# A fused attention and mixer block on one core: attention in 57-query blocks of 64 keys, large weights in pieces between the transposes, and a searched order of the blocks

## The chip, the cores and the metric

The kernel runs on one core of one Trainium2 chip. The metric is device time in microseconds (us), from runs most of which agree within 1.5%. The profiled execution is described by its *span*, which is about 2 us shorter than the time of the same run. "PE" is TensorE, "PEld" its weight loads, "DVE" VectorE, "ACT" ScalarE, "POOL" GpSimd and "SP" the engine whose queue issues nearly all DMAs. The *granted clock* is the share of full speed that TensorE was given. A run more than 1.5% above the fastest of its kernel is called slow here. The medians quoted are of all runs of a kernel.

## The reference

The input is `x` with 2048 tokens of 448 values, and all data are bf16. Two pre-norm blocks follow each other.

```python
def A(x, wqkv, wo):            # 16 heads of 28, window 8, dilation 2
    q, k, v = split(x @ wqkv)
    idx = pos[:, None] - arange(8)[None, :] * 2      # keys s, s-2, ..., s-14
    logits = einsum("bhsd,bhswd->bhsw", q, k[idx]) * 28**-0.5     # masked where idx < 0
    return einsum("bhsw,bhswd->bhsd", softmax(logits), v[idx]) @ wo

def B(x, w1, w2, w3, w4):      # w1, w2: 448x448, w3: 448x1792, w4: 1792x448
    h  = gelu(layernorm(x) @ w1)
    hs = shift_quarters(h) @ w2        # quarters of the columns moved by +1, -1, +2, -2 tokens
    x1 = x + hs
    return x1 + gelu(layernorm(x1) @ w3) @ w4

h  = x + A(layernorm(x), wqkv, wo)
h2 = h + B(layernorm(h), w1, w2, w3, w4)
```

## The kernel before

Because of the dilation, even and odd tokens never meet in the attention. The kernel keeps them apart as two "parities" (`a`) of 1024 positions, each query then seeing its own and the 7 keys before. Normalized tiles are transposed by DMA on the SP queue (`HT<-ln` in the trace) and feed the projections.

A block of the attention has 121 queries and 128 keys, so that the keys fill the partitions. Most of the 128x121 scores lie outside the window. They are computed and exponentiated, and then multiplied by a 0/1 mask. The four heads of a group use the four 32-row strips of the array.

```python
NQ = 121
def phase_att(g):                       # two windows w, one group c of four heads at a time
    for (c, a, w), o in cols.items():   # scores, 28 x 128 keys by 121 queries
        k0 = W0 + NQ * w - 7
        for j in range(4):
            ins.append(mm(Ts[j // 2](...), QK[r, 1, a, c, k0:k0 + nk], QK[r, 0, a, c, q0:q0 + nq], True, True))
    for jp in range(2):
        act(pj, Ts[jp](...), ACT.Exp, 2 * tot, scale=SCALE)
        dve("tensor_tensor", ..., out=pj, in0=pj, in1=mb, op=ALU.mult)      # the mask
    for (c, a, w), o in cols.items():   # probabilities times values, 128 keys by 32
        for j in range(4):
            ins.append(mm(T(...), vt[0:nk, w % NV, a, 4 * c + j, :], pt[0:nk, sl, j, o:o + nq], True, True))
    ...                                 # copy out, then norm(): denominators through DRAM, product
```

The weights are issued in one go, after the first four layer norms. W3 is two DMAs of 1568 KB and W4 is one of the same size:

```python
def weights():
    ...                                                    # wo, w1, w2
    wload("w3", w3_s[:], B_w3)
    dma("w4", w4_s[:], B_w4.rearrange("(f k) n -> k f n", k=128), D * F * 2)

setup()
for m in range(4): phase_LN1(m)
weights()
unit_qkv(0); phase_att(0); unit_qkv(1); ...
```

Nothing of this runs in program order. The program text builds a list of operations with durations, and a list scheduler in the kernel orders them for each engine. Of the ready operations it takes the one that can start first in its own model of the chip. Among operations that could start within a slack of that, it takes the one with the lower `prio`, which before the change is the place in the program text. All instructions are emitted by one helper, so every one carries the same line number in the profile, and groups are told apart by their tiles.

Of the kernel before, what the change touches and what calls it, by code (L numbers as in the profile page):

```python
# [15 lines left out]
class _Op:  # L16
    __slots__ = ("idx", "eng", "ins", "kw", "dur", "deps", "users", "sem", "val", "t0", "t1", "clock", "is_dma",
                 "chan", "lat", "odeps", "tag", "opts", "table", "prio", "groups", "mode", "xb")

    def __init__(self, idx, eng, ins, dur):  # L20
        self.idx = idx; self.eng = eng; self.ins = ins; self.dur = dur
        self.deps = set(); self.users = 0; self.sem = None; self.val = 0
        self.t0 = None; self.t1 = None; self.clock = None; self.xb = False
        self.opts = None; self.table = None; self.prio = idx; self.groups = []; self.mode = None
        self.is_dma = False; self.chan = None; self.lat = 0.0; self.odeps = set()
# [61 lines left out]
class _Sched:  # L87
# [11 lines left out]
    def macro(self, eng, ins, dur, chan=None, lat=0.0, opts=None, table=None, mode=None, after=()):  # L99
# [3 lines left out]
        if chan is not None:  # L103
            op.is_dma = True; op.chan = chan; op.lat = float(lat)
            self.chan_count[chan] = self.chan_count.get(chan, 0) + 1
            op.val = 16 * self.chan_count[chan]
# [62 lines left out]
    XLAT = 130.0  # L169
    TABLE = 1300.0  # L170
    MODE = 90.0

    def prepare(self):
# [16 lines left out]
        self.engs = sorted(set(e for op in self.ops for e in (op.opts or {op.eng: None})))  # L190

    def schedule(self, dma_bw=180.0, slack=100.0):
        if not hasattr(self, "children"):
            self.prepare()
        n = len(self.ops)
        children = self.children
        npend = list(self.npend)
        XLAT = self.XLAT
        ops = self.ops
        engs = self.engs  # L200
        holder = [None] * 8
        held_by = [[] for _ in range(8)]
        fin = [0.0] * n
        arr = [{} for _ in range(n)]
# [4 lines left out]
        def place(n, t, taken=()):  # L209
            best = None  # L210
            for b in range(0, 8, n):
                f = 0.0
                for x in range(b, b + n):
                    if holder[x] is not None or x in taken:
                        break
                    for o in held_by[x]:
                        if o.eng != "pe":
                            v = fin[o.idx] + XLAT
                            if v > f:
                                f = v  # L220
                else:
                    key = (max(f, t), 0 if n > 1 else -b, -f)
# [5 lines left out]
        base = [dict.fromkeys(engs, 0.0) for _ in range(0)]  # L228

        def push(op):  # L230
            at = {}
            for e in (op.opts or (op.eng,)):
                t = 0.0
                for d in op.deps:
                    i = d.idx
                    x = fin[i] + (0.0 if d.is_dma or eng_of[i] == e else XLAT)
                    if x > t:
                        t = x
                for d in op.odeps:
                    i = d.idx  # L240
                    if fin_start[i] > t and eng_of[i] != e:
                        t = fin_start[i]
# [4 lines left out]
        fin_start = [0.0] * n  # L247
# [8 lines left out]
        dma_free = 0.0  # L256
        done = 0
        MODE = self.MODE
        cands = {e: None for e in engs}
        dirty = set(engs)  # L260
        while done < n:
            best = None
            for e in engs:
                cand = None
                fr = free[e]
                for op in ready[e]:
                    st = arr[op.idx][e]
                    if st < fr:
                        st = fr
                    if cand is not None and st > cand[0] + slack:  # L270
                        continue
                    bad = False
                    if op.groups and e == "pe":
                        taken = ()
                        for g in op.groups:
                            if g not in gbank:
                                at = place(g.n, st, taken)
                                if at is None:
                                    bad = True
                                    break  # L280
                                if at[1] > st:
                                    st = at[1]
                                taken = taken + tuple(range(at[0], at[0] + g.n))
                        if bad:
                            continue
                    if e == "act" and op.table is not None and op.table != table:
                        st += self.TABLE
                    if cand is None or st < cand[0] - slack or (st < cand[0] + slack and op.prio < cand[1].prio):
# [11 lines left out]
            if e == "act" and op.table is not None:  # L300
                table = op.table
            if e == "pe":
                if op.mode != mode:
                    dur += MODE
                mode = op.mode
            op.t0 = st
            fin_start[i] = st
            for g in op.groups:
                if g not in gbank:
# [4 lines left out]
                    g.wait = set()  # L314
                    for x in range(b, b + g.n):
# [3 lines left out]
                    g.opener = op  # L319
                gleft[g] -= 1  # L320
                b = gbank[g]
                for x in range(b, b + g.n):
# [3 lines left out]
            if op.is_dma:  # L326
                free[e] = st + dur
                ts = max(st + dur, dma_free)
                dma_free = ts + op.lat / dma_bw
                op.t1 = dma_free + 2000.0  # L330
            else:
                op.t1 = st + dur
                free[e] = op.t1
# [4 lines left out]
            for ch in children[i]:  # L338
# [5 lines left out]
        return order  # L344
# [52 lines left out]
def _fast_path(nc, es, flag, A_x, A_wqkv, A_wo, B_w1, B_w2, B_w3, B_w4, out):  # L397
# [3 lines left out]
    NF, KB, NQ, W0 = 14, 7, 121, 8  # L401
# [16 lines left out]
    HT = sb("HT", [128, KB, 16 + 1024], BF16)  # L418
    QK = sb("QK", [128, 2, 2, 4, QW], BF16)
    NV = 5  # L420
    vt = sb("vt", [128, NV, 2, 16, 32], BF16)
    pt = sb("pt", [128, 3, 4, 4 * NQ], BF16)
    osb = sb("osb", [128, 3, 2, 512], F32)
    rzb = sb("rzb", [128, 2, 512], F32)
    zp = sb("zp", [128, 3, 32], F32)
    rzp = sb("rzp", [128, 3, 32], F32)
    msk = sb("msk", [128, 4 * NQ], BF16)
    xin = sb("xin", [128, 16, D], BF16)
    xb = sb("xb", [128, 16, D], BF16)
    NL = 3  # L430
# [16 lines left out]
    rz_d = nc.dram_tensor("rz_scratch", (9 * 4, 1024), F32, kind="Internal")  # L447

# [16 lines left out]
    def dma(chan, out_ap, in_ap, nbytes, dur=500.0):  # L465
        return S.add("sp", "dma_start", dur, chan=chan, lat=nbytes, out=out_ap, in_=in_ap)
# [16 lines left out]
    def wload(chan, dst, src):  # L483
        for u in range(2):
            dma(chan + "ab"[u], dst[half[u]], src.rearrange("(b k) n -> k b n", k=64),
                src.shape[0] * src.shape[1] * 2)
# [7 lines left out]
    def load_x(m):  # L494
        dma("x%d" % m, xin[:, 2 * m:2 * m + 2, :].rearrange("p a n -> p (a n)"), xrows(A_x, m), 128 * D * 4)

    def setup():
        S.tag = "setup"
        for m in range(2):
            load_x(m)  # L500
        for b0, b1 in ((0, 3), (3, 7)):
            wload("wqk%d" % b0, wst[:, b0:b1, :], A_wqkv[64 * b0:64 * b1, 0:2 * D])
        wload("wv", wv_s[:], A_wqkv[:, 2 * D:3 * D])
        for m in range(2, 8):
            load_x(m)
        pool("memset", 300, ap=mhalf[:], constant=-0.5)
        dve("memset", 100, ap=HT[:, :, 0:16], constant=0.0)
        dve("memset", 100, ap=QK[:, 1, :, :, 0:W0], constant=0.0)
        dve("memset", 100, ap=QK[:, 1, :, :, W0 + 1024:QW], constant=0.0)
        dve("memset", 400, ap=vt[:, :, :, :, 29:32], constant=0.0)  # L510
        dve("memset", 200, ap=vt[:, :, :, :, 28], constant=2.0 ** -4)
        dve("memset", 100, ap=vt[0:7, 0, :, :, 28], constant=0.0)
        dve("memset", 600, ap=msk[:], constant=1.0)
        m4 = msk[:].rearrange("p (b q) -> p b q", q=NQ)
        pool("affine_select", 600, out=m4, in_=m4, pattern=[[0, 4], [-1, NQ]], compare_op=ALU.is_ge, fill=0.0, base=0,
             channel_multiplier=1)
        pool("affine_select", 600, out=m4, in_=m4, pattern=[[0, 4], [1, NQ]], compare_op=ALU.is_ge, fill=0.0, base=7,
             channel_multiplier=-1)
        dve("memset", 70, ap=ones[:], constant=1.0)
        dve("memset", 70, ap=w1_s[:, KB * D:], constant=0.0)  # L520
        dve("memset", 1100, ap=osb[:], constant=1.0)
        dve("memset", 500, ap=wqk_p[:, :, :, 28:32], constant=0.0)
        pool("memset", 1600, ap=wo_s[:], constant=0.0)
        for c in range(4):
            for w in range(2):
# [3 lines left out]
                    "act": ([("activation", dict(ka, func=ACT.Copy))], 220 + 784 / 1.2),  # L529
                    "dve": ([("tensor_copy", ka)], 560)}, **ka)  # L530

    def weights():
        S.tag = "weights"
        wov = A_wo.rearrange("(c j d) n -> j d c n", c=4, j=4)
        for j in range(4):
            dma("wo%d" % j, wo_s[32 * j:32 * j + 28, :, :], wov[j], D * D * 2 // 4)
        wload("w1", w1_s[:, 0:KB * D].rearrange("p (b n) -> p b n", b=KB), B_w1)
        dma("w2", w2_s[:], B_w2.rearrange("(c k) n -> k c n", k=112), D * D * 2)
        wload("w3", w3_s[:], B_w3)
        dma("w4", w4_s[:], B_w4.rearrange("(f k) n -> k f n", k=128), D * F * 2)  # L540
# [3 lines left out]
    def ln_stats(kind, src, i):  # L544
        k = stc[0] % 8
        stc[0] += 1
        dve("bn_stats", 600, out=st6[:, k, :], in_=src)
        dve("bn_aggr", 180, out=mv[:, kind, i, :], in_=st6[:, k, :])

    def inv_std(slot, kind, i0, n, s1=1.0, s2=EPS):  # L550
        pool("tensor_scalar", 250, out=vtmp[:, slot, i0:i0 + n], in0=mv[:, kind, i0:i0 + n, 1], scalar1=s1,
             scalar2=s2, op0=ALU.mult, op1=ALU.add)
        pool("tensor_tensor", 400 + 164 * n, out=rstd[:, slot, i0:i0 + n], in0=vtmp[:, slot, i0:i0 + n],
             in1=mhalf[:, 0:n], op=ALU.pow)

    def normalize(slot, kind, i, out_ap, in_ap):
        dve("tensor_scalar", 400, out=out_ap, in0=in_ap, scalar1=mv[:, kind, i, 0:1],
            scalar2=rstd[:, slot, i:i + 1], op0=ALU.subtract, op1=ALU.mult)

    lctr = [0]  # L560

    def ln_to_HT(slot, kind, m, src):
        sl = lctr[0] % NL
        lctr[0] += 1
        for a in range(2):
            normalize(slot, kind, 2 * m + a, ln[:, sl, :, a, :], src[:, 2 * m + a, :].rearrange("p (b d) -> p b d", d=64))
        S.add("sp", "dma_start_transpose", 1400.0, chan=ch("tr"), lat=128 * 896 * 2,
# [765 lines left out]
```

## Time and profile before

| | before |
|---|---|
| time, median of 3 runs | 285.08 us |
| span of the profiled run | 280.3 us |
| first matmul | 21.6 us |
| PE busy | 192.5 us |
| PE idle between the first and the last matmul | 61.2 us |
| after the last matmul | 5.0 us |
| mean granted clock | 0.884 |

The head of the page of the kernel before: span, busy time by engine, then the busy tenths of PE and the granted clock in 40 slices of 7 us each.

```profile
span 280.3 us, 5851 instructions
...
PE 192.5 (69%) x2567; PEld 128.4 (46%) x2567; DVE 138.4 (49%) x296; ACT 102.0 (36%) x109; POOL 51.3 (18%) x92
...
PE   0009640699906540999999935569996489999892
...
PEclk9999955599986796699999977599999669999999
```

PE is the busiest engine. It is idle in the first three slices and has holes at slices 5 to 8, 12 to 16, 24 to 27 and 31 to 32, counted from 1. Below many of the holes, or just after them, the clock row drops to 5 to 7, so the idle time costs twice, since the work after it runs slower.

The waits of the kernel before, PE only: who ended the idle time, us in total, how many times, the longest.

```profile
PE ps L1259 <- DMA HT<-ln: 42.2, 3, 21.6
PE ps L1259 <- DVE pt L1259: 13.7, 6, 7.1
...
PE ps L1259 <- issue: 3.4, 2, 2.1
```

The transposes (`HT<-ln`) ended 42.2 us of PE's idle time in three waits, of which 21.6 us is the start. The masked probabilities (`DVE pt`) ended 13.7 us. The normalized attention (not shown) ended another 7.8 us.

The timeline of the kernel before: first of the SP queue, then of PE (start, length, what ran, and in brackets the idle time before it and what ended it).

```profile
24.72 27.08 SPq L1259 DMA_TRANSPOSE HT<-ln  x3
```

```profile
51.84 2.80 PE L1259 MATMUL ps<-wv_s,HT 64*128 64x448 bf16 x14 [9.75 <-DMA HT<-ln]
...
61.00 1.49 PE L1259 MATMUL ps<-wv_s,HT 64*128 64x448 bf16 x14
```

Three transposes issued from 24.7 us on kept the SP queue for 27.08 us (the first of them for 23.01), and most single ones later in the same trace take 1.22 to 1.25 us. They stood behind W3 and W4. The page lists those loads as three of 1568 KB with a median of 23.2 us to landing. The second and third lines show the value projection of a window after that wait, and the same work later. It took 2.80 us against 1.49 us, which is the price of a cold clock. The Trainium skill's page "TensorE: Matmul & The Clock Gate", Part 1, says the array runs at half clock until it has been busy for some 3.4 us. This pair, 1.9 to 1, agrees with the half clock.

The groups of the attention in the kernel before (line, engine, operation, tiles, shapes, count, busy us, mean ns, idle before).

```profile
L1259 ACT ACTIVATE pt<-ps 128x968 bf16<-128x968 f32 (+1 forms) x34 | 31.0, 976 | 6.5 <-PE ps L1259 6.5
L1259 DVE TENSOR_TENSOR pt<-pt,msk 128x968 bf16<-128x968 bf16 (+1 forms) x34 | 22.0, 653 | 24.8 <-ACT pt L1259 24.8
L1259 PE MATMUL ps<-pt,vt 128*32 128x121 bf16 (+1 forms) x288 | 8.1, 247 | 15.8 <-DVE pt L1259 13.7 <-ACT pt L1259 2.1
L1259 PE MATMUL ps<-QK 28*128 28x121 bf16 (+1 forms) x288 | 7.4, 226 | 3.0 <-DVE osb L1259 0.8 <-ACT pt L1259 0.7 <-ACT vt L1259 0.7
```

Exponentials and masks cost 31.0 us of ACT and 22.0 us of DVE. Those engines are busy 36% and 49% of the span.

### The profile page before, as it was taken

Reading aid. Unit: us, or ns where it says so; the run is one execution under the profiler, and the core shown is the slowest. Engines: PE = TensorE matmul, PEld = TensorE weight load, DVE = VectorE, ACT = ScalarE, POOL = GpSimd, SP = SyncE. Lnnn points to the kernel's source line nnn. Section 1 sums busy time; section 2 is a strip of 40 time slices with the busy share of each in tenths; the row PEclk is TensorE's granted clock in tenths of the full one; section 3 lists DMA queues with packets and bytes.
Section 4 is the critical chain, followed back from the end, with each engine's and each line's share of the span. In section 5 each row is a group of like instructions: output and inputs, shape, how many; then the busy total and the mean of one; then the engine's idle time right before and its main releaser. Section 6 shows DMA issues by size and latency. Waiting matters only on the chain.

```text
span 280.3 us, 5851 instructions
## 1 busy us (share of the span) xinstructions
PE 192.5 (69%) x2567; PEld 128.4 (46%) x2567; DVE 138.4 (49%) x296; ACT 102.0 (36%) x109; POOL 51.3 (18%) x92
## 2 busy tenths in 40 slices
PE   0009640699906540999999935569996489999892
PEld 0006420377505220765865622269553439857651
DVE  6857180207897587174824466682127764020020
ACT  0403870169653600236971670026201105603500
POOL 4414000000040023016400001731002547000000
PEclk9999955599986796699999977599999669999999
DMA  6999999822044234203110132321010313001001
GB/s 176 218 284 211 218 204 278 145 79 77 7 105 62 61 82 103 73 1 69 35 36 33 37 83 77 75 57 35 2 47 19 68 33 62 10 33 35 4 34 41
DMA packets 35341, 23.16 MB, mean 83 GB/s; under 512 B 25836, under 2 KB 33388, under 8 KB 35308
## 3 DMA queue, kind: packets, MB, share of 16 engines
q1 hardware_dynamic: 35308, 22.71, 35.8%
q8 instruction: 22, 0.36, 0.6%
q14 instruction: 11, 0.09, 0.1%
HBM read 15.09 MB, written 1.97 MB: 61 GB/s over the span
## 4 chain that ended last, share of the span: by engine, by line
PE 59%; DMA 17%; DVE 11%; ACT 6%; issue 3%; POOL 2%; SPq 1%; DVEq 0%
PE ps L1259 59%; DMA HT<-ln 15%; DVE st L1259 3%; ACT pt L1259 3%; DVE xb L1259 2%; DMA h<-in_A_wqkv_dram 2%; DVE xin L1259 2%; DVE QK L1259 1%; ACT QK L1259 1%; POOL rstd L1259 1%; SPq L1259 1%; DVE mv L1259 1%; DVE ln L1259 1%; ACT osb L1259 1%; ACT L1259 0%
## 5 line engine op out<-in xcount | busy, mean ns | idle before, releaser
L1259 PE MATMUL ps<-HT,w_s 64*128 64x256 bf16 (+1 forms) x1064 | 61.7, 279 | 19.2 <-DMA HT<-ln 10.8
L1259 PEld LDWEIGHTS ps<-HT,w_s 64*128 64x128 bf16 x1064 | 55.2, 101 | 25.8 <-DMA HT<-ln 16.2
L1259 DVE TENSOR_TENSOR xb<-ps,xb 128x448 bf16<-128x448 f32 (+1 forms) x24 | 18.6, 776 | 64.0 <-PE ps L1259 64.0
L1259 ACT ACTIVATE QK<-ps 128x1024 bf16<-128x1024 f32 (+2 forms) x24 | 22.7, 953 | 53.2 <-PE ps L1259 53.2
L1259 POOL TENSOR_SCALAR vtmp<-mv 128x2 f32<-128x2 f32 (+1 forms) x34 | 7.9, 233 | 175.2 <-DVE mv L1259 174.0
L1259 PE MATMUL ps<-wv_s,HT 64*128 64x448 bf16 (+1 forms) x126 | 17.1, 423 | 32.2 <-DMA HT<-ln 31.3
L1259 DVE TENSOR_TENSOR pt<-pt,msk 128x968 bf16<-128x968 bf16 (+1 forms) x34 | 22.0, 653 | 24.8 <-ACT pt L1259 24.8
L1259 ACT ACTIVATE pt<-ps 128x968 bf16<-128x968 f32 (+1 forms) x34 | 31.0, 976 | 6.5 <-PE ps L1259 6.5
L1259 ACT ACTIVATE arena<-ps 128x1024 bf16<-128x1024 f32 x14 | 14.3, 1023 | 37.4 <-PE ps L1259 37.4
L1259 PE MATMUL ps<-HT,arena 64*128 64x256 bf16 x448 | 26.3, 273 | 0.4 <-ACT QK L1259 0.4
L1259 PEld LDWEIGHTS ps<-wv_s,HT 64*128 64x128 bf16 (+1 forms) x126 | 6.8, 109 | 39.3 <-DMA HT<-ln 31.6
L1259 POOL TENSOR_TENSOR rstd<-vtmp,mhalf 128x2 f32<-128x2 f32 (+1 forms) x34 | 24.1, 709 | 2.8
L1259 PEld LDWEIGHTS ps<-HT,arena 64*128 64x128 bf16 x448 | 21.9, 96 | 4.9 <-issue 0.9
L1259 PE MATMUL ps<-w_s,arena 128*128 128x448 bf16 x112 | 21.5, 353 | 1.1 <-ACT arena L1259 1.1
L1259 PE MATMUL ps<-w_s,h 128*128 128x448 bf16 x112 | 21.5, 353 | 0.5 <-ACT h L1259 0.5
L1259 DVE TENSOR_SCALAR ln<-xin,mv,rstd 128x448 bf16<-128x448 bf16 x32 | 14.7, 496 | 12.4 <-DMA HT<-ln 9.5
L1259 DVE BATCH_NORM_STATS2 st<-xin 128x6 f32<-128x448 bf16 x32 | 19.3, 603 | 3.1 <-DMA xin<-in_A_x_dram 2.9
L1259 PE MATMUL ps<-wo_s,QK 128*128 128x448 bf16 x64 | 14.6, 385 | 7.8 <-DVE QK L1259 7.8
L1259 PE MATMUL ps<-w_s,QK 112*128 112x448 bf16 x64 | 17.6, 444 | 2.4 <-ACT QK L1259 2.4
L1259 ACT ACTIVATE h<-ps 128x1024 bf16<-128x1024 f32 x14 | 14.1, 1024 | 13.7 <-PE ps L1259 13.7
L1259 PE MATMUL ps<-pt,vt 128*32 128x121 bf16 (+1 forms) x288 | 8.1, 247 | 15.8 <-DVE pt L1259 13.7
L1259 POOL TENSOR_TENSOR xb<-xb,xin 128x448 bf16<-128x448 bf16 x16 | 16.2, 1030 | 6.9 <-DVE ln L1259 6.9
(44 smaller groups left out, 149.3 us busy)
## 6 DMA issues: line engine op xcount, KB each, us to landing
w_s<-in_B_w_dram SPq DMA_DIRECT2D x3, 1568.0 KB, 23.2
rzb<-rz_scratch SPq DMA_DIRECT2D x32, 128.0 KB, 2.7
xin<-in_A_x_dram SPq DMA_DIRECT2D x8, 224.0 KB, 10.6
out_dram<-xb SPq DMA_DIRECT2D x8, 224.0 KB, 2.0
w_s<-in_B_w_dram SPq DMA_DIRECT2D x3, 392.0 KB, 6.6
h<-in_A_wqkv_dram SPq DMA_DIRECT2D x2, 448.0 KB, 7.7
wv_s<-in_A_wqkv_dram SPq DMA_DIRECT2D x2, 392.0 KB, 10.4
h<-in_A_wqkv_dram SPq DMA_DIRECT2D x2, 336.0 KB, 5.2
```

The lines of the kernel that those rows point to most:

```text
L1259: inst = getattr(eng, meth)(**kw)
```

## The change

The change has five parts.

1. **Attention blocks of 57 queries and 64 keys**, two of them on the two partition halves. A pass still fills the 128 partitions, and each query is scored against 64 keys instead of 128, of which 8 count. There are 18 passes instead of 34 on ACT and DVE, while PE makes 576 score and 576 value matmuls instead of 288 and 288.
2. **The first loads** are split over the SP and ACT queues, with fewer bytes ahead of the first transpose.
3. **W3 in 14 pieces of 224 KB and W4 in two of 784 KB**, each issued only once a given transpose has been issued.
4. **A re-measured cost model** in the scheduler, products of the normalization that may go to DVE or POOL, a double buffer for the denominators and pairwise layer-norm statistics.
5. **A searched precedence**: each block has a rank, found offline by a search over the scheduler's own model, and the rank replaces the program order in the choice among ready operations.

```diff
-    NF, KB, NQ, W0 = 14, 7, 121, 8
+    NF, KB, NQ, W0 = 14, 7, 57, 8
 # ---- values: four 64x64 quadrants of the array
-                ins.append(mm(T(lambda p, a=a: p[0:n, a, 0:D]), HT[half[a], b, k0:k0 + n], wv_s[half[a], b, :],
-                              b == 0, b == 6))
+            for h in range(2):
+                for a in range(2):
+                    k0 = 16 + NQ * (2 * t + h) - 7
+                    ins.append(mm(T(lambda p, a=a, h=h: p[half[h], a, 0:D]), HT[half[a], b, k0:k0 + 64], wv_s[half[a], b, :],
+                                  b == 0, b == 6))
 # ---- attention: two blocks h on the partition halves
+                        for j in (2 * jp, 2 * jp + 1):
+                            r = slice(32 * j, 32 * j + 28)
+                            ins.append(mm(T(lambda p, j=j, h=h, k=k: p[half[h], j % 2, NQ * k:NQ * k + NQ]),
+                                          QK[r, 1, a, c, q0 - 7:q0 + NQ], QK[r, 0, a, c, q0:q0 + NQ], True, True))
+                pj = pt[:, sl, 2 * jp:2 * jp + 2, 0:tot]
+                act(pj, T(lambda p: p[:, :, 0:tot]), ACT.Exp, 2 * tot, scale=SCALE)
 ...
 # ---- loads
+        dma("wva", wv_s[half[0]], wvv, D * D * 2, 620, after=trs[1:2])
+        for m in range(4, 8):
+            load_x(m, after=trs[1:2])
 ...
-        wload("w3", w3_s[:], B_w3)
-        dma("w4", w4_s[:], B_w4.rearrange("(f k) n -> k f n", k=128), D * F * 2)
+        for b in range(KB):
+            wload("w3", w3_s[:, b:b + 1, :], B_w3[64 * b:64 * b + 64, :], after=trs[3:4], bulk=True)
+        for f in range(2):
+            dma("w4_%d" % f, w4_s[:, 7 * f:7 * f + 7, :], B_w4[896 * f:896 * f + 896, :]..., D * F,
+                740, rate=350.0, after=trs[5:6], bulk=True)
 ...
 # ---- order
+    rank = {b: k for k, b in enumerate((
+        "V_1 V_2 LN3_5 QK_1_0 QK_0_1 norm_0_3 LN2_3 QK_0_3 LN2_4 QK_1_1 QK_1_2 att_1_0 WO_7 QK_0_0 att_0_1 "
+        ...
+    ).split())}
+    for op in S.ops:
+        op.prio = 10000 * rank[op.tag] + op.idx
```

## The prediction

> **What bounds the kernel.** The page shows TensorE (PE) busy 192.5 of 280.3 us. Costed with the timeline's durations at full clock, its work is about 170 us (estimate): query/key projection 16 x 1.53, values 9 x 1.4, attention 34 x 0.33, output projection 8 x 1.52, W1 12.4, W2 8 x 1.52, W3 28 x 1.53, W4 16 x 2.65. So the span splits into 170 warm PE work, 22.5 of the same work at a lower clock, 21.6 before the first matmul, 5.0 after the last, and 61 of PE idle between. The Trainium skill ("TensorE: Matmul & The Clock Gate", Part 1) says the array runs at half clock until it has been busy for about 3.4 us; the trace agrees: 14 matmuls of a value window took 2.80 us after an idle stretch at 51.8 us and 1.49 us when warm.
>
> The idle time (waits, timeline): transposes 42.2 us (three waits: 21.6 at the start, 9.75 at 51.8, 10.9 at 112.4), masked probabilities 13.7 (7.1 of it at 85.6), normalized attention 7.8. The transpose issued at 24.7 us sat until 51.8 us: it was behind the W3 and W4 loads (1568 KB pieces, median landing 23.2 us) and the first for 4 MB. In the stretches 75-112, 165-185 and 212-231 us PE is busy for only 14.5 of 37, 10.5 of 20 and 11.9 of 19 us; there VectorE chains (layer norm, denominators) and transposes are critical.
>
> **What the change does.**
> 1. Attention blocks of 57 queries and 64 keys, two on the partition halves, nearly halve the score area: exp passes 34 -> 18 (31.0 -> 17 us ScalarE), mask products 34 -> 18 (22.0 -> 11.5 us VectorE), output copies 17 -> 9 of double size (10.6 -> 9). PE pays: 576 -> 1152 small matmuls (the tail's 32 took 0.35-0.44 us), so 11 -> 14-15 us. Values stay near 1.35 us each if four quadrants of the array stream together, which no line of this trace shows.
> 2. Fewer bytes (about 2.9 instead of 4.2 MB) precede the first transpose, on two queues: first matmul at 15-16 us instead of 21.6.
> 3. W3/W4 come in pieces after transposes: a transpose waits for one piece, not for 4.7 MB. The 9.75 us stall goes.
> 4. The searched order with re-measured durations, movable products: projection and attention are pulled forward, so the layer-norm chains hide under W3/W4 (85 us of PE work). In-order queues will still stall.
>
> Critical-path sum, after (us): warm PE 173.5, first matmul 15.5, lower clock 10, idle between 22, tail 5: span 226. The time was 2-5 us over the span before: **229 us**, range 213 to 247 (8 in 10). Faster by over 2%: 0.97; within 2%: 0.02; slower: 0.01. ScalarE and VectorE savings pay only in the attention stretches.
>
> **Checks in the profile.** Step 1: exp and mask groups x18 at 0.93 and 0.63 us; PE busy 180-190 us. Step 2: first matmul at 14-17 us. Step 3: no PE wait for a transpose over 5 us after the start. Step 4: no 20-us stretch after 60 us with PE under 70%; granted clock over 0.93.
>
> **What would make it wrong.** Transposes that still wait for all pieces in flight, so the head stays near 20 us and W3 arrives late (240-250). 64x64 matmuls that don't overlap (values +12 us, scores +6). Chains left exposed by a search on wrong durations (+15 us). A nearly gapless PE from 16 us gives about 210.

## The result, and the profile after

The kernel after takes 229.77 us, the median of four runs from 229.01 to 232.17, against 285.05 us for the kernel before in the same session. The ratio is 0.8101, with a 95% interval of 0.8006 to 0.8195. Ratios here are the mean time of one kernel's fast runs over that of the other's of the same rounds, so they are not quite the ratio of the quoted medians.

The head of the page of the kernel after, with the same rows as before.

```profile
span 227.5 us, 7213 instructions
...
PE 183.9 (81%) x3269; PEld 126.4 (56%) x3269; DVE 109.1 (48%) x254; ACT 90.3 (40%) x98; POOL 64.9 (29%) x106
...
PE   0009997399793879866769999999999999999990
...
PEclk9999999769999558999999999999999999999999
```

A slice is now 5.7 us long. PE is idle for three of them, then busy with some holes until slice 21, and full from there to the last one. The waits of PE in the kernel after, then two of the transposes that follow the fourth, from its SP queue:

```profile
PE ps L1285 <- ACT arena L1285: 17.0, 1, 17.0
PE ps L1285 <- issue: 7.4, 5, 3.2
PE ps L1285 <- POOL QK L1285: 6.8, 2, 4.2
PE ps L1285 <- DMA HT<-ln: 3.5, 3, 1.8
```

```profile
25.85 2.58 SPq L1285 DMA_TRANSPOSE HT<-ln  x2
```

The 17.0 us is the start. The transposes, which cost 42.2 us before with the start in it, end only 3.5 us of waits now, and none of the first eight holds the SP queue for more than 1.92 us. Two other waits stand out in the list. One is for POOL, which now makes some of the products that normalize the attention (6.8 us). The other, called `issue`, is time in which PE waited for nothing that the profile shows (7.4 us, 3.4 before).

Windows of the kernel after, the one from 119 to 222 us (length, then busy us of PE, PEld, DVE, ACT and POOL with their counts, the granted clock, DMA share and GB/s):

```profile
119.00:222.00 103.00, 102.90 (x1225) 71.29 (x1225) 42.75 (x101) 33.86 (x34) 26.25 (x44) 1.00 0.18 42
```

For the last 103 us before the tail PE never stops. The kernel before had stretches with PE busy only 14.5 of 37 us (75 to 112), 10.5 of 20 (165 to 185) and 11.9 of 19 (212 to 231), while layer-norm chains ran on DVE. Such chains now run beside the large matmuls of W3 and W4. The order is needed for that: in the last 103 us before the tail PE is idle for 0.1 us here, for 8.5 us in a1 below, which lacks the ranks, and for 16.4 us in the kernel before.

| us | before | after | difference | predicted after |
|---|---|---|---|---|
| until the first matmul | 21.6 | 17.0 | -4.6 | 15.5 |
| PE idle between | 61.2 | 21.2 | -40.0 | 22 |
| PE busy, at full clock (estimate) | 170 | 172 to 174 | +2 to +4 | 173.5 |
| PE busy, extra at the lower clock (estimate) | 22.5 | 10 to 12 | -10.5 to -12.5 | 10 |
| after the last matmul | 5.0 | 5.4 | +0.4 | 5 |
| span | 280.3 | 227.5 | -52.8 | 226 |

Busy and idle times are read from the profile. The split of the busy time into full and lower clock is an estimate from the durations of the same work warm and cold in the timeline.

The groups of the attention in the kernel after:

```profile
L1285 ACT ACTIVATE pt<-ps 128x912 bf16<-128x912 f32 x18 | 15.9, 940 | 3.4 <-PE ps L1285 3.4
L1285 DVE TENSOR_TENSOR pt<-pt,msk 128x912 bf16<-128x912 bf16 x18 | 13.1, 738 | 20.5 <-ACT pt L1285 20.5
L1285 PE MATMUL ps<-QK 28*64 28x57 bf16 x576 | 7.2, 194 | 5.4 <-issue 3.6 <-ACT osb L1285 1.7
L1285 PE MATMUL ps<-pt,vt 64*32 64x57 bf16 x576 | 6.5, 203 | 4.7 <-issue 3.8 <-DVE pt L1285 0.8
```

ACT does half the passes at about the same cost each. The mask product saves less, because one pass of 128x912 takes 738 ns while the larger 128x968 took 653 in the mean; why is not shown. The means of PE's small matmuls are durations that overlap. The busy time of scores and values together is 13.7 us, against 15.5 us before, with twice as many matmuls. So PE did not pay for them in busy time. Whether it paid in `issue` stalls is taken up below.

The timeline of PE in the kernel after:

```profile
16.96 5.83 PE L1285 MATMUL ps<-HT,arena 64*128 64x256 bf16 x56 [16.96 <-ACT arena L1285]
...
32.34 1.52 PE L1285 MATMUL ps<-wv_s,HT 64*64 64x448 bf16 x28
...
38.14 0.48 PE L1285 MATMUL ps<-pt,vt 64*32 64x57 bf16 x40
40.43 0.90 PE L1285 MATMUL ps<-pt,vt 64*32 64x57 bf16 x88 [1.81 <-issue]
41.26 0.83 PE L1285 MATMUL ps<-QK 28*64 28x57 bf16 x40
45.25 0.53 PE L1285 MATMUL ps<-QK 28*64 28x57 bf16 x24 [3.17 <-issue]
```

The value projection in four quadrants takes 1.52 us for 28 matmuls, as against 1.49 us for the 14 larger ones before, both covering nearly the same tokens. The Trainium skill's page "TensorEngine Tiling (Array Packing)", Tiling Modes, says that the 64x64 mode gives four independent tiles, and here they do run side by side. The last lines show something new. A burst of `pt,vt` matmuls stops after 40, waits 1.81 us for `issue`, and goes on with 88. Then 40 of the next kind run, and PE stops again for 3.17 us. From stop to stop there are 88 + 40 = 128 matmuls, in the middle of bursts whose operands were ready.

### The profile page after: what moved, and what is told of

Read it like the earlier page. It is cut to its first block, busy times and chain, and to the rows that moved or that the text cites. A ratio compares the mean times of both kernels' runs of the same rounds, so it can differ in the third digit from the quotient of the medians.

```text
span 227.5 us, 7213 instructions
## 1 busy us (share of the span) xinstructions
PE 183.9 (81%) x3269; PEld 126.4 (56%) x3269; DVE 109.1 (48%) x254; ACT 90.3 (40%) x98; POOL 64.9 (29%) x106
## 4 chain that ended last, share of the span: by engine, by line
PE 64%; DMA 15%; DVE 6%; issue 4%; ACT 4%; SPq 3%; POOL 2%
PE ps L1285 64%; DMA h<-in_A_wqkv_dram 5%; DMA xb<-rz_scratch 4%; SPq L1285 3%; DMA HT<-ln 2%; DMA rzb<-rz_scratch 2%; DMA rz_scratch<-rzp 2%; DMA zp<-osb 1%; POOL QK L1285 1%; ACT arena L1285 1%; ACT osb L1285 1%; DVE xb L1285 1%; DVE st L1285 1%; DVE ln L1285 1%; DVE xin L1285 1%
## 5 line engine op out<-in xcount | busy, mean ns | idle before, releaser
L1285 PE MATMUL ps<-HT,w_s 64*128 64x256 bf16 (+1 forms) x1064 | 56.1, 264 | 3.5 <-DMA HT<-ln 3.5
L1285 PEld LDWEIGHTS ps<-HT,w_s 64*128 64x128 bf16 x1064 | 49.1, 94 | 10.8 <-DMA HT<-ln 4.1
L1285 ACT ACTIVATE QK<-ps 128x1024 bf16<-128x1024 f32 (+2 forms) x26 | 24.9, 960 | 22.6 <-PE ps L1285 22.5
L1285 POOL TENSOR_SCALAR vtmp<-mv 128x2 f32<-128x2 f32 x32 | 6.5, 203 | 73.5 <-DVE mv L1285 72.2
L1285 POOL TENSOR_TENSOR rstd<-vtmp,mhalf 128x2 f32<-128x2 f32 x32 | 22.3, 696 | 2.7
L1285 DVE TENSOR_TENSOR pt<-pt,msk 128x912 bf16<-128x912 bf16 x18 | 13.1, 738 | 20.5 <-ACT pt L1285 20.5
L1285 PE MATMUL ps<-w_s,h 128*128 128x448 bf16 x112 | 21.9, 353 | 0.0
L1285 PE MATMUL ps<-wo_s,QK 128*128 128x448 bf16 x64 | 15.7, 408 | 6.8 <-POOL QK L1285 6.8
L1285 ACT ACTIVATE pt<-ps 128x912 bf16<-128x912 f32 x18 | 15.9, 940 | 3.4 <-PE ps L1285 3.4
L1285 POOL TENSOR_TENSOR xb<-xb,xin 128x448 bf16<-128x448 bf16 x16 | 16.4, 1051 | 1.9 <-DVE ln L1285 1.9
L1285 PEld LDWEIGHTS ps<-w_s,h 128*128 128x128 bf16 x112 | 10.9, 98 | 10.3 <-issue 0.2
L1285 PEld LDWEIGHTS ps<-w_s,arena 128*128 128x128 bf16 x112 | 10.9, 98 | 10.2
L1285 PEld LDWEIGHTS ps<-wo_s,QK 128*128 128x128 bf16 x64 | 6.6, 108 | 14.7 <-issue 7.5
L1285 PE MATMUL ps<-wv_s,HT 64*64 64x448 bf16 x252 | 13.8, 352 | 0.0
```

The costliest lines, as they stand in the source:

```text
L1285: inst = getattr(eng, meth)(**kw)
```

## The experiments

Theory **O** says that the gain comes from the order and from what lets it work (head, pieces), and that the smaller attention area is worth little because ACT and DVE have slack. Its rival **A** says that the attention area is the main thing. The experiments take parts out of the kernel after (a1 to a3) and put parts alone into the kernel before (b1 to b3). Two more look at the `issue` stalls (a3d, a3e), and two try for something better (c1, c2).

### The order: program order in the kernel after (a1)

```diff
-    rank = {b: k for k, b in enumerate(("V_1 V_2 LN3_5 ...").split())}
-    for op in S.ops:
-        op.prio = 10000 * rank[op.tag] + op.idx
```

> The kernel after, with the searched precedence taken out: blocks keep the order in which the program lists them. Theory O (the 55 us come mainly from what the precedence and the placing of loads let overlap): 240 to 258 us, with new PE idle time of 10 us or more after 60 us. Rival A (the gain is mainly the halved score area: fewer exp and mask passes): within 4 us of 230.

It took 251.66 us, ratio 0.8883 (0.8823 to 0.8942). That is 21.9 us more than the kernel after (22.3 by the ratios, times 285), from the ranks alone. The waits of PE in it, and one line of its timeline:

```profile
PE ps L1274 <- DMA HT<-ln: 27.9, 3, 16.8
...
PE ps L1274 <- DVE QK L1274: 12.4, 1, 12.4
```

```profile
121.87 3.17 PE L1274 MATMUL ps<-wo_s,QK 128*128 128x448 bf16 x8 [12.39 <-DVE QK L1274]
```

In program order PE waits 12.39 us at once for a normalized attention tile before an output projection, and 11 us more for transposes after the start. Those waits are where layer-norm and denominator chains had no PE work beside them. PE's `issue` waits grew as well, from 7.4 to 13.6 us in six, the longest 5.4. The clock is back at 0.888.

### The pieces: W3 and W4 whole again in the kernel after (a2)

```diff
-        for b in range(KB):
-            wload("w3", w3_s[:, b:b + 1, :], B_w3[64 * b:64 * b + 64, :], after=trs[3:4], bulk=True)
+        wload("w3", w3_s[:], B_w3, after=trs[3:4])
-        for f in range(2):
-            dma("w4_%d" % f, ..., D * F, 740, rate=350.0, after=trs[5:6], bulk=True)
+        dma("w4", w4_s[:], ..., D * F * 2, 740, rate=350.0, after=trs[3:4])
```

> The kernel after, with W3 and W4 loaded whole (2 x 1568 KB and 1568 KB) as soon as the fourth transpose has been issued, not in pieces. If large loads hold up the transposes behind them, as theory O says of the stall at 24.7 to 51.8 us of before: 242 to 255 us, and a PE wait for a transpose of 8 us or more between 25 and 60 us. If only the bytes matter: within 3 us of 230.

The edit also moves W4, which the kernel after issues behind the sixth transpose, to behind the fourth, and the ranks stay those that were searched for the pieces. So it tests the pieces and their place together. It took 245.08 us, ratio 0.8673 (0.8598 to 0.8747), 15.3 us more than the kernel after (16.3 by the ratios). The time is as expected, but the view that was named is not. Three lines, from the SP queue, from PE's timeline and from its waits:

```profile
24.71 20.16 SPq L1282 DMA_TRANSPOSE HT<-ln  x3
```

```profile
39.03 0.64 PE L1282 MATMUL ps<-QK 28*64 28x57 bf16 x31 [5.63 <-issue]
```

```profile
PE ps L1282 <- issue: 15.6, 6, 5.6
PE ps L1282 <- DMA HT<-ln: 7.1, 3, 5.0
```

The three transposes were held up as before, for 20.16 us; with the pieces (25.85 us, above) two took 2.58. PE's waits for a transpose, though, came to 7.1 us, the longest 5.0, and the larger new part is `issue`, 15.6 us instead of 7.4, with a longest stall of 5.63 us while the large loads were moving. One reading is that PE's own instructions come through the DMA engines and queue behind the same large loads. It fits this stall, which at the same place in the instruction stream lasted 0.45 us in the kernel after. But it was not tested by itself, and whole loads are not needed for a stall of that length: with the pieces, a1 has one of 5.40 us and c2 one of 5.12. The Trainium skill's page "DMA: Bandwidth & Descriptors", section "Issuing engines are not separate DMA queues", says that DMAs started by different engines run on the same 16 DMA engines and interleave there. It does not speak of instructions, and since the loads and the transposes here come from one queue, SP's, no run here tests it.

### The attention: 121-query windows in the kernel after (a3), with the order searched again

```diff
-    NF, KB, NQ, W0 = 14, 7, 57, 8
+    NF, KB, NQ, W0 = 14, 7, 121, 8
     # phase_V, phase_att and norm of the kernel before, with the movable products,
     # the double denominator buffer and the DMA durations of the kernel after
-    phase_att(0)
+    phase_att(0)
+    phase_att(1)
     ...                                  # likewise 2, 3 and 4 where 1 and 2 stood
-    rank = (searched for 57)
+    rank = (searched for 121, in the same scheduler model)
```

> The kernel after, with the attention of before (121 queries by 128 keys, 34 exp and 34 mask passes, four heads' scores in one batch), its block precedence searched anew for it in the kernel's own scheduler. Theory O: 232 to 243 us, since ScalarE and VectorE have idle time. Rival A: 255 to 275 us.

It took 227.02 us, ratio 0.803 (0.7966 to 0.8093), below what either theory expected. It was run again on one chip beside the unchanged kernel after, in five rounds each.

> The kernel after once more, on one chip with the next two, to compare it directly with the 121-query version and the try for a faster one: 229 to 231 us.

> The 121-query version in the same rounds. If the 57-query blocks gain anything in this schedule: over 231 us. If they gain nothing and cost stalls of the instruction stream: 225 to 228 us, that is 1 to 2% faster than the kernel after.

The kernel after took 228.37 us, ratio 0.8043 (0.8011 to 0.8075), and the 121-query kernel 225.82 us, ratio 0.7964 (0.7928 to 0.8000). The intervals do not overlap. The smaller attention area is not the source of the gain, and with an order searched for each it costs about 1%. Each was searched once, so a luckier search could shift so small a difference; c1 and c2 below, a second pair, point the same way. A line of the page and one of the waits of a3 (of its first run) show how:

```profile
PE 182.5 (82%) x2567; PEld 121.0 (54%) x2567; DVE 125.7 (56%) x275; ACT 103.5 (46%) x115; POOL 65.5 (29%) x103
```

```profile
PE ps L1301 <- DVE pt L1301: 11.1, 4, 6.1
```

ACT is busy 103.5 us instead of 90.3 and DVE 125.7 instead of 109.1. With 46% and 56% of the span they still have slack. PE waits 11.1 us for masked probabilities, which the 57-query blocks cut to 0.8. But there is no `issue` line at all in its waits (one of 0.5 us in its second profile), and the first output projection starts at 66.3 us instead of 74.8, because a group holds 242 query positions instead of 456. So the change traded one wait for others of the same size. The scheduler's own model gets this comparison wrong. Run again for each kernel, it puts the span at 197.4 us for the 57-query blocks and 202.8 for the 121-query windows, a preference of 5.4 us for the former, while the measured spans are 227.5 and 223.4. The search had no reason to look elsewhere.

### The attention alone in the kernel before (b3)

```diff
-    NF, KB, NQ, W0 = 14, 7, 121, 8
+    NF, KB, NQ, W0 = 14, 7, 57, 8
     # phase_V, phase_att and norm of the kernel after; single denominator buffer, products on DVE
     # program order; att(0) where att(1) stood, att(1) after unit_qkv(3), att(2) where att(4) stood
```

> The kernel before, with only the attention changed (57-query blocks, groups of 456 queries, so each attention stage comes one unit of projections later than before), its own scheduler and loads kept. Theory O: no gain, 280 to 320 us, because the larger group postpones the first output projection and the stalls on transposes stay. Rival A: 245 to 268 us. Exp and mask passes should be 18 in either case.

It took 317.81 us, ratio 1.1174 (1.1095 to 1.1253), so this part alone makes the kernel slower by 33 us. The waits of PE in it:

```profile
PE ps L1246 <- DMA HT<-ln: 58.9, 6, 20.9
PE ps L1246 <- DVE QK L1246: 29.4, 3, 13.5
```

The first output projection starts at 101.3 us instead of 75.0, since the first group now needs a second unit of projections, and everything behind it is later. Larger groups need an order that puts other work into the gap.

### The pieces alone in the kernel before (b1)

```diff
-        wload("w3", w3_s[:], B_w3)
-        dma("w4", w4_s[:], ...)
+    # counted from 0: W3 pieces 0 to 2 after transpose 5, pieces 3 and 4 after 6, 5 and 6 after 7; W4 in two after 8
```

> The kernel before, with one change: W3 in 14 pieces of 224 KB and W4 in 2 of 784 KB, each issued after a given later transpose, instead of whole loads ahead of them. Theory O: the stall of three transposes at 24.7 to 51.8 us goes, 262 to 276 us, no transpose issue over 5 us after 25 us. Rival P (the pieces pay only together with the searched order): within 4 us of 285.

It took 275.5 us, ratio 0.9666 (0.9587 to 0.9744), a gain of about 9.5 us (0.0334 x 285) and at the small end of what was expected. The SP queue, then PE's timeline:

```profile
22.66 10.62 SPq L1278 DMA_TRANSPOSE HT<-ln  x4
```

```profile
35.15 3.23 PE L1278 MATMUL ps<-HT,arena 64*128 64x256 bf16 x56 [0.47 <-ACT pt L1278]
...
73.42 0.60 PE L1278 MATMUL ps<-pt,vt 128*32 128x121 bf16 x16 [7.21 <-DVE pt L1278]
...
96.73 5.91 PE L1278 MATMUL ps<-HT,w_s 64*128 64x256 bf16 x56 [9.68 <-DMA HT<-ln]
```

The transposes go through by 33.3 us, and the projections of the second unit start at 35.15 us instead of behind the value window at 51.84, which is some 17 to 19 us earlier. The two long waits that follow, 7.21 us for masked probabilities and 9.68 us for a transpose, are not new: the kernel before has them at 85.56 us (7.09) and 112.42 us (10.85). Behind the second the lead is still 15.7 us. It is lost later and falls to 5.7 us by 179.57 us, in part through new waits of 2.80 us for a transpose (120.16) and 4.98 us for masked probabilities (154.52). So most of what the early transposes win is given back in this order.

### The first loads alone in the kernel before (b2)

```diff
-            wload("wqk%d" % b0, wst[:, b0:b1, :], A_wqkv[64 * b0:64 * b1, 0:2 * D])
+            wload("wqk%d" % b0, wst[:, b0:b1, :], A_wqkv[64 * b0:64 * b1, 0:2 * D], ("sp", "act"))
+        load_x(2, "act")
+        load_x(3, "act")
+        dma("wvb", wv_s[half[1]], wvv, D * D * 2, q="act")
 ...
+    dma("wva", wv_s[half[0]], wvv, D * D * 2, after=trs[1:2])      # x4 to x7 and all other weights likewise
```

> The kernel before, with only its first loads changed: half of the query/key weights, two x tiles and half of the value weights on ScalarE's queue, the other value half and four x tiles after the second transpose. The first matmul should come at 16 to 18 us instead of 21.6. If the head is on the critical path through: 279 to 281 us. If the later stall of the transposes behind W3 and W4, which ends when all bytes have landed, swallows it: within 2 us of 285.

It took 276.27 us, ratio 0.9707 (0.9636 to 0.9779), a gain of about 8.4 us (0.0293 x 285) that neither theory expected. The SP queue:

```profile
17.27 1.24 SPq L1267 DMA_TRANSPOSE HT<-ln  x1
...
28.74 24.07 SPq L1267 DMA_TRANSPOSE HT<-ln  x2
```

The first matmul starts at 17.36 us, 4.2 us earlier than before, as in the kernel after. But the edit did more. It also let the third and fourth transposes go at 17.27 and 21.87 us, ahead of W3 and W4, so two units of projections could run early. The two after them still sit for 24.07 us behind the weights. This run therefore does not measure the start alone.

The parts alone give -9.5, -8.4 and +33 us, which does not come near the -55 us of the whole. All the parts without the ranks (a1) give about -33. A likely reading is that the searched order needs the early transposes to have something to choose from, and that the early transposes need the order to keep what they win. The order was not tried in the old kernel, so only the second half of this is seen, in b1.

### The issue stalls: doubled and tenfold bursts (a3d, a3e)

Theory **I** says that a long burst of small matmuls runs through its instructions faster than they are brought in. The 121-query kernel a3 has no such stalls. If the theory holds, repeating its small matmuls without adding any other work should bring them about (the repeated matmuls write the same result, so the output stays correct).

```diff
 # a3d
-            pe(ins, len(cols) * 54, "r32", after=av_ops[-2:-1])
+            pe(ins + ins, len(cols) * 54, "r32", after=av_ops[-2:-1])
-            av_ops.append(pe(ins, len(cols) * 54, "c32"))
+            av_ops.append(pe(ins + ins, len(cols) * 54, "c32"))
 # a3e
-            av_ops.append(pe(ins, len(cols) * 54, "c32"))
+            av_ops.append(pe(ins * 10, len(cols) * 54, "c32"))
```

> The 227-us kernel with 121-query windows, each score and value-product matmul of the attention issued twice (the second overwrites with the same result): 1152 small matmuls as the 57-query version has, with the area and passes of before. Theory I (in bursts of small matmuls PE outruns its instruction fetch, and this cost the 57-query version its gain): PE waits labelled issue of 4 us or more in mid-burst, where the single version has none, and 232 to 245 us. If the stalls came from the 64-column tiles or from weight traffic alone: no issue waits over 1 us in bursts, and under 232 us.

> Not a candidate: the 121-query version with each value-product batch issued ten times (160 small matmuls in a row, the same result), to measure long bursts by themselves. Theory I (instructions come in blocks of 128 weight-load and matmul pairs, and a burst faster than the fetch stalls at their ends): waits labelled issue of 0.5 to 5 us inside most of the 17 bursts, 128 matmuls apart in one burst where two fall in it, also after 100 us where little else is on the DMA queues. If the stalls belong to 64-column tiles or to weight traffic: none after 100 us. The time should be 255 to 300 us.

The doubled kernel took 227.24 us (fast runs 226.9 and 223.75) and had no `issue` wait in its profile, which is of a slow run. The expectation of theory I missed, and the rival's was met. Its bursts were only 32 to 64 long, at some 17 to 20 ns for each matmul, so a3e makes the bursts longer; it has no 64-column tiles. The tenfold kernel took 279.09 us in its one look, whose state is unknown, so only the kind of its waits is used here. The waits of PE in it, and its timeline near the end of the attention:

```profile
PE ps L1301 <- issue: 22.4, 17, 2.7
```

```profile
146.48 1.21 PE L1301 MATMUL ps<-pt,vt 63*32 63x56 bf16 x128 [0.40 <-issue]
150.21 1.21 PE L1301 MATMUL ps<-pt,vt 63*32 63x56 bf16 x86 [2.52 <-issue]
```

There are 17 stalls with 22.4 us in total, as theory I expected: 14 in the repeated products and 3 in projections, and seven of them after 100 us. In these two lines PE stops, runs 128 matmuls, and stops again for 2.52 us. A matmul here is two instructions, a weight load and the product, so 128 of them are 256 instructions. The page also has a queue named `instruction`, of this kernel, the kernel after and a3 in turn:

```profile
q8 instruction: 41, 0.67, 1.0%
```

```profile
q8 instruction: 26, 0.43, 0.8%
```

```profile
q8 instruction: 21, 0.34, 0.7%
```

These are packets, MB and share, so a packet is about 16.4 KB. The kernel after has 3269 matmuls and as many weight loads, 6538 instructions or 25.5 times 256, and the queue has 26 packets. a3 has 5134 instructions, 20.1 times 256, and 21 packets. The tenfold kernel has 10318, 40.3 times 256, and 41. This fits one packet for each 256 instructions of PE, to within one: the kernel before has 22 with as many instructions as a3, a1 has 27. The places of the stalls settle more. All PE records of each trace were counted in order: weight loads, matmuls and the few semaphore and control instructions. All 46 `issue` waits of the kernel after, a1, a2, b3, c2 and a3e then begin 193 to 195 records past a multiple of 256, wherever that falls in a burst. The two of the kernel before do not (23 and 68), so they are of another kind. The Trainium skill's page "Runtime: NRT & Kernel Launch", section "Instruction fetch mechanics", says that instructions come in blocks of 16 KiB or 256 instructions and that the crossing is mostly hidden. The runs agree on the size of the block. They do not agree that it is hidden for bursts like these, at 9.5 ns a matmul (1.21 us for 128). So it is shown that the stalls stand at one fixed place in every 256 instructions of PE, as the ends of blocks would. That what PE waits for there is the fetch is inferred; no view names it, and why one such place costs nothing, another 0.4 us and another 5 stays open.

### A warm start and a corrected model (c1, c2)

c1 is a3 with three more edits, and c2 is the kernel after with the same three. First, both halves of the value weights and the tiles `x2` to `x7` are loaded on SP behind the second transpose, so that less is in flight ahead of it. Second, 22 matmuls that nobody reads run on the first normalized tile while the first transposes are under way. Third, the order is searched again in a changed model, which has one shared pipe for all DMAs, transposes that wait for what is in flight, and half clock for PE during 3.4 us after it has been idle. In c2 the model also charges 17 ns instead of 12.5 for a small matmul.

```diff
+    def warm_up(n):
+        pe([mm(T(lambda p: p[:, 0, 0:448]), lw[:, 0:128], lw[:, 0:448], True, True) for _ in range(n)], n * 189.2, "full")
 ...
-        load_x(2, "act")
-        load_x(3, "act")
-        dma("wvb", wv_s[half[1]], wvv, D * D * 2, 620, q="act")
+        for m in range(2, 8):
+            load_x(m, after=trs[1:2])
```

> A try at a faster kernel: 121-query windows, value weights and x tiles 2 and 3 after the second transpose, 22 idle matmuls on the first normalized tile to raise the clock before the first real one, and the order searched anew in a scheduler whose model has one shared DMA pipe and the half clock after idle time. First matmul of the projection at 13 to 15 us at full clock; 212 to 222 us. If the model's DMA and clock terms don't matter: 224 to 230 us.

> The kernel after (57-query blocks) with the same first loads, idle matmuls and re-searched order as the 223-us kernel; its model charges 17 instead of 12.5 ns per small matmul. If the smaller area is worth something once the order is as good: under 221 us. If it is worth nothing: 222 to 228 us, with issue waits of 3 us or more.

c1 took 223.03 us, ratio 0.7834 (0.7753 to 0.7915). Its fast runs are at 222.01 to 223.55 us and its first projection at 15.32 us. Both are just outside what was expected (212 to 222 us, 13 to 15 us), but the kernel beats the two others. Its timeline of PE at the start:

```profile
8.39 7.00 PE L1324 MATMUL ps<-ln 128*128 128x448 bf16 x22 [8.39 <-DVE ln L1324]
15.32 3.23 PE L1324 MATMUL ps<-HT,arena 64*128 64x256 bf16 x56
```

The same 56 projection matmuls that took 5.83 us at the start of the kernel after take 3.23 us here, because the clock is already up, and they start 1.6 us earlier. How the gain over a3 (223.03 us against 225.82 to 227.02, from other chips) divides between the loads, the warm-up and the new order is not separated.

c2 took 227.43 us, ratio 0.8031 (0.7988 to 0.8074), which is not told apart from the kernel after on the same chip (0.8011 to 0.8075). It has 11.0 us of `issue` stalls in seven, the longest 5.1, as the second of its expectations said. They may have taken what the warm start gave; that was not measured apart. c1, on the larger windows, has none. The changed model, run again, now puts c1 at 202.7 us and c2 at 205.5, so it ranks the two as the chip does, perhaps through its 17 ns for a small matmul in c2 alone. This supports the reading that the stalls are the price of the small blocks. Whether 57-query blocks would win in a kernel without them is not shown.

## Why the prediction was right or wrong

The prediction of 229.0 us with a range of 213 to 247 was right: 229.77 us. Term by term:

- **The bound.** The account of the span before (170 us of work at full clock, 22.5 of slowdown, 61 of idle between, 21.6 and 5.0 at the ends) gave a sum after of 226 us, and the span was 227.5. The idle time between was predicted at 22 and came to 21.2, the lower clock at 10 and came to 10 to 12 (estimate). a1 shows that the order is worth 22 us by itself, as step 4 said in kind.
- **Step 1, the attention area.** The counts and the exponentials were right (18 passes of 940 ns). The mask product was undersized, 738 ns instead of 630, so 13.1 us instead of 11.5. PE was predicted to pay 3 to 4 us for twice the matmuls (from 11 to 14 or 15). Its busy time for them was 13.7 us against a measured 15.5 before, so it paid nothing there. The values took 1.52 us each instead of 1.35, far from the 12 us more that was feared, so the four quadrants do overlap. The closing sentence of the step, that these savings pay only in the attention stretches, was right in direction. But it did not say what the runs show, which is that the whole step is worth nothing or about -1% in the final kernel, and costs 33 us in the old order.
- **Step 2, the start.** The first matmul came at 17.0 us. That lies in the range given for the check (14 to 17) but not at the 15 to 16 us that the sum used. So 1.5 us was missing there.
- **Step 3, the pieces.** The check holds, since no wait for a transpose after the start is over 1.8 us. a2 shows that the pieces and their place are worth 15.3 us in the final order, more than the 9.75 us stall that the step named. Only 3.6 us of the added waits there are for transposes, and 8.2 us are `issue`, which the step did not foresee.
- **Step 4, the order.** The granted clock was 0.954 in the profiled run, as predicted over 0.93 (0.927 to 0.954 in the four runs). The check that no stretch of 20 us after 60 us has PE under 70% failed narrowly. From 99 to 119 us PE was busy 13.3 us of 20, or 66%.
- **What was not foreseen.** The `issue` stalls, 7.4 us, have no term in the sum. They are inside the 21.2 us of idle time, so the other waits came to 13.8 us where 22 were allowed for. The point value was good partly by luck in this. The stalls were not among the reasons given for being wrong.

What stays open: the gain of the re-measured durations, the movable products and the double buffer alone, the searched order in the old kernel, how much of a2 is the size of the loads and how much their place, the split of c1's gain, and whether the stalls under large loads (a2) come from the DMA engines that both share.

## What to carry to other kernels

Before the work of an engine is cut, ask whether that engine is waited for: here half the exponentials and masks went away and the time did not follow, while a changed precedence of the same instructions was worth 22 us, and splitting two weights and placing the pieces 15 us. Parts of such a change do not add up, so test them by taking them out of the whole as well as by putting them alone into the old kernel. A search is only as good as the costs its model charges: a model that knew nothing of instruction stalls and of loads ahead of transposes chose the blocks that the chip liked less.

## What the Trainium skill lacked or had wrong

- "Runtime: NRT & Kernel Launch", section "Instruction fetch mechanics", calls the crossing of a 16 KiB block mostly hidden. In and behind bursts of small tiled matmuls PE stalled at one fixed place in every 256 instructions, for 0.4 to 3.2 us each and 7.4 us in total in the kernel after, up to 5.4 us each and 13.6 us in total in a1, up to 5.6 us each and 15.6 us in total in a2, and 22.4 us in 17 stalls with tenfold bursts.
- "DMA: Bandwidth & Descriptors", section "Rules for kernel authors", gives no cost for a DMA transpose behind large loads. Here three of them took 27.08 us behind three loads of 1568 KB, as against 1.22 to 1.25 us for a free one.
- "TensorEngine Tiling (Array Packing)", section "Instruction Overhead", gives each matmul an overhead of about 60 cycles. That section gives no rate for tiles side by side. In a3e 128 such matmuls of 56 columns took 1.21 us, 9.5 ns each, and what then stopped PE was, by the places of the stalls, probably the supply of instructions. No page names that limit for tiled work.
- "DMA: Bandwidth & Descriptors", section "Rules for kernel authors", advises at least 1 MiB per DMA for bandwidth. It does not say what such loads cost the transfers behind them. In this kernel, 14 pieces of 224 KB and two of 784 KB, all placed between the transposes, beat three loads of 1568 KB by 15.3 us.
